# A decode-attention and MLP kernel: down-projection as partial sums per column tile, fewer VectorE instructions, and a final weight piece split by columns

## The chip, the cores and the metric

The kernel runs on one core of a Trainium2 chip. The metric is the device time of one execution in microseconds (us). A "span" is the length that the profile of one execution shows; it is 1.4 to 1.9 us shorter than the device time of the same execution. All kernels that ran gave correct results.

## The reference

```python
g = sigmoid((x * gate_w).sum(-1, keepdims=True))          # x: 8 x 1 x 576
q = x @ wq                                                 # 8 batches, 32 heads of 128
a = softmax(q @ k_cache^T * 128**-0.5) @ v_cache @ wo      # 4096 keys per head
b = gelu(layernorm(x) @ w1 + b1) @ w2 + b2                 # 576 -> 4608 -> 576
return g * a + (1 - g) * b
```

The K and V caches are the work: 2 x 8 x 32 x 4096 x 128 values in bfloat16, 537 MB of the 557 MB that the kernel reads.

## The kernel before

The kernel cuts the attention into 32 groups (eight heads of one batch each). A group needs one K load and one V load of 8.4 MB. SBUF has room for three such slots. The loads are issued by SyncE on one queue, strictly in order, and each one waits until its slot is free:

| order | load | slot | free when |
|---|---|---|---|
| 1-3 | wq, w1, w2 | 0, 1, 2 | at once |
| 4 | K0 | 0 | the q projection has read wq |
| 5 | K1 | 1 | the up-projection has read w1 |
| 6 | V0 | 2 | the down-projection has read w2 |
| 7 | K2 | 0 | TensorE has summed the last chunk of K0 |
| 8 | V1 | 1 | TensorE has summed the last chunk of K1 |
| 9 | K3 | 2 | the output of V0 has been evicted |

The order of TensorE's work at the start is: up-projection, then (after gelu on VectorE and ScalarE) 36 small matmuls that transpose the hidden row, then (after four VectorE copies of it) the down-projection, then the two matmuls that broadcast q of group 0, and only then the attention.

```python
    for k in range(3):                       # up-projection, w1 in slot 1
        for c in range(4):
            ...
    free[1] = [p_up]
    ...                                      # gelu on VectorE and ScalarE
    for j in range(NJ):                      # NJ = 36: transposes of the hidden row
        p_hT = op("tensor", ...)
    v_hT = [op("vector", lambda e, c=c: e.tensor_copy(
        out=hT_sb[32 * c:32 * c + 32, :, :], in_=ht_ps[0:32, :, c, :]), [p_hT]) for c in range(4)]

    def quarters(lhsT, w, first, stop, waits):          # 4 matmuls of 144 columns into y_ps
        for i in range(4):
            last = op("tensor", lambda e, i=i: e.matmul(
                y_ps[32 * i:32 * i + B, 0:QN], lhsT=lhsT, rhs=w[:, i * QN:(i + 1) * QN], start=first, stop=stop),
                waits if i == 0 else ())
        return last

    for jt in range(NJ):                     # down-projection, w2 in slot 2
        p_down = quarters(hT_sb[:, jt, :], w2_sb[:, jt, :], jt == 0, False, ...)
    for i in range(4):
        p_b2 = op("tensor", ...)             # bias b2 times (1 - g)
    free[2] = [p_b2]
    ...
    q_of(0)                                  # first q: 2 matmuls on TensorE, then a copy on ScalarE
    next_load()                              # K1
    next_load()                              # V0
    ...
    for g in range(NG):
        scores(g, between)                   # 8 x (VectorE multiply K by q, TensorE sums, VectorE reduce)
        free[n_of["k", g]] = [... p_sum[g, NCK - 1]]    # in the loop: a later matmul of the same point
        next_load()
        ...                                  # softmax, P @ V, eviction
```

At the end, y (already holding the MLP part) gets the wo product in three pieces of rows, `WO = ((0, 24), (24, 30), (30, 32))`, and four copies bring it to SBUF for the output.

Of the kernel before, what the change touches and what calls it, by code (L numbers as in the profile page):

```python
# [6 lines left out]
ALU = mybir.AluOpType  # L7
AX = mybir.AxisListType
BF16 = mybir.dt.bfloat16
F32 = mybir.dt.float32  # L10

B = 8
D = 576
# [6 lines left out]
NJ = F // 128  # L20

HB = 8
# [10 lines left out]
QN = D // 4  # L33
QP = 96 + B
# [3 lines left out]
NDQ = 4  # L38
NJO = H * DH // 128
# [4 lines left out]
class Stream:  # L44
# [13 lines left out]
    def op(self, engine, fn, waits=(), dma=None, token=None):  # L58

        rec = {"fn": fn, "waits": [w for w in waits if w is not None], "value": None, "inc": None, "token": None}  # L60
        self.ops[engine].append(rec)
        if dma is not None:
            rec["inc"] = (dma[0], 16)
            return ("dma", *dma)
        if token is not None:
            key = (engine, token)
            if key not in self.tok:
                self.tok[key] = self.nc.alloc_semaphore(f"tok_{engine}_{token}")
                self.given[key] = 0
            self.given[key] += 1  # L70
            rec["inc"] = (self.tok[key], 1)
            rec["token"] = (token, self.given[key])
        return ("op", engine, rec)
# [117 lines left out]
def bass_gated_mix__mha_block_cached__mixer_channel_mlp__decode_kernel(  # L191
# [16 lines left out]
    sb = nc.alloc_sbuf_tensor  # L208
    S = Stream(nc)
    op = S.op  # L210

    def pstride(t):
        return t[tuple([slice(None)] * len(t.shape))].ap[0][0]
# [16 lines left out]
    w2_sb = view(SL, 2 * SLOT, [128, NJ, D])  # L230
# [33 lines left out]
    late = Tail(2, NJ * D)  # L264
    b1_row = late.take([1, F])
    hrow = late.take([128, FC])
    hT_sb = late.take([128, NJ, B])
    b2_8 = late.take([B, D])
    b2_f = late.take32([B, D])
    t2 = late.take32([128, FC])  # L270
# [4 lines left out]
    selq = sb("selq", [128, TQ, HB * NDQ], F32)  # L275
    zs = sb("zs", [32, 1], F32)
    acc = sb("acc", [128, GL, HB], F32)
    OTs = sb("OTs", [32, NJO, GL], F32)
# [9 lines left out]
    one1 = sb("one1", [1, B], BF16)  # L288
    diag2 = sb("diag2", [B, 2, B], F32)
    g4 = sb("g4", [128, 2], F32)  # L290
    g32 = sb("g32", [32, 2, B], F32)
    ident = sb("ident", [128, 128], BF16)
    hneg = sb("hneg", [128, HB], F32)
    sel32 = sb("sel32", [128, HB, TQ], F32)
# [3 lines left out]
    mB = sb("mB", [128, 32], F32)  # L298
    mC = sb("mC", [128, 32], F32)
    mD = sb("mD", [128, 32], F32)  # L300
# [3 lines left out]
    O_sb = sb("O_sb", [128, TQ, DH], F32)  # L304
    rz = sb("rz", [128, 1], F32)

# [9 lines left out]
    g4_ps = bank[3][:, 0:2]  # L316
    g32_ps = bank[3][0:32, 64:64 + 2 * B]
    ht_ps = PS[:, 0:NJ * 32].rearrange("p (j c b) -> p j c b", j=NJ, c=4)
    xt_ps = bank[7]
    YT_COL = 64  # L320
# [4 lines left out]
    def load(engine, dst, src, name, waits=()):  # L325
        return op(engine, lambda e: e.dma_start(dst, src), waits, dma=(nc.alloc_semaphore(name), 16))
# [5 lines left out]
    def bcast(t, at, n):  # L332
        return bass.AP(tensor=t.tensor, offset=t.offset + at, ap=[[0, B], [1, n]])
# [15 lines left out]
    ld_b1 = load("scalar", b1_row, bass.AP(tensor=B_b1.tensor, offset=B_b1.offset, ap=[[F, 1], [1, F]]), "ld_b1")  # L349
    ld_b2 = load("scalar", b2_8, bcast(B_b2, 0, D), "ld_b2")  # L350

# [38 lines left out]
    def memset(engine, ap, value):  # L390
# [14 lines left out]
                                                    base=PH - 1, pattern=[[PH, HB], [0, NDQ]], channel_multiplier=-1), [t])  # L405
    c_hneg = op("vector", lambda e: e.tensor_scalar(out=hneg[:, :], in0=hsel[:, ::NDQ], scalar1=-1.0, scalar2=60000.0,
                                                    op0=ALU.add, op1=ALU.mult), [c_hsel])
# [8 lines left out]
        axis=AX.X, op=ALU.add), [c_id])  # L416
    c_selq = op("vector", lambda e: e.tensor_copy(
        out=selq[:].rearrange("p t (h q) -> p t h q", q=NDQ),
        in_=bass.AP(tensor=sel32, offset=0, ap=[[pstride(sel32), 128], [1, TQ], [TQ, HB], [0, NDQ]])), [c_sel32])
    c_one8 = memset("gpsimd", ones8[:], 1.0)  # L420
    c_one1 = memset("gpsimd", one1[:], 1.0)
    c_b2 = op("gpsimd", lambda e: e.tensor_copy(out=b2_f, in_=b2_8), [ld_b2])
    c_sp8 = op("vector", lambda e: e.tensor_copy(
        out=spread8[:].rearrange("b (c r) -> b c r", c=4),
        in_=bass.AP(tensor=ident, offset=0, ap=[[pstride(ident), B], [0, 4], [1, 32]])), [c_id])
    c_Rows = op("vector", lambda e: e.tensor_reduce(
        out=Rows[:], in_=ident[:, :].rearrange("p (h r) -> p h r", h=4), axis=AX.X, op=ALU.add), [c_id])
    c_Sel = op("vector", lambda e: e.tensor_copy(
        out=Sel[:].rearrange("p (h r) -> p h r", h=4),
# [35 lines left out]
    def untransposed(dst, col, waits):  # L465
        return op("vector", lambda e: e.tensor_copy(
            out=dst.rearrange("p k b -> p (k b)"), in_=xt_ps[:, col:col + (NKF + 2) * B]), waits)
# [8 lines left out]
                                                   scalar1=-1.0, scalar2=1.0, op0=ALU.mult, op1=ALU.add), [a_g])  # L476
    v_dg = op("vector", lambda e: e.tensor_tensor(
        out=diag2[:], in0=bass.AP(tensor=ident, offset=0, ap=[[pstride(ident), B], [0, 2], [1, B]]),
        in1=bass.AP(tensor=stat, offset=G_COL, ap=[[pstride(stat), B], [1, 2], [0, B]]), op=ALU.mult), [v_omg, c_id])
    v_yz = spread(yz, y_sb, [v_y])  # L480
# [3 lines left out]
           [v_dg, c_sp8])  # L484
    t = op("tensor", lambda e: e.matmul(g32_ps, lhsT=ones8[:, :], rhs=diag2[:].rearrange("k s b -> k (s b)"),
                                        start=True, stop=True), [c_one8])
    v_g4 = op("vector", lambda e: e.tensor_copy(out=g4[:, :], in_=g4_ps), [t])
    v_g32 = op("vector", lambda e: e.tensor_copy(out=g32[:].rearrange("p s b -> p (s b)"), in_=g32_ps), [t])

# [50 lines left out]

    def quarters(lhsT, w, first, stop, waits):

        for i in range(4):
            last = op("tensor", lambda e, i=i: e.matmul(  # L544
                y_ps[32 * i:32 * i + B, 0:QN], lhsT=lhsT, rhs=w[:, i * QN:(i + 1) * QN], start=first, stop=stop),
                waits if i == 0 else ())
        return last

    for jt in range(NJ):
        p_down = quarters(hT_sb[:, jt, :], w2_sb[:, jt, :], jt == 0, False,  # L550
                          [ld_w2, *v_hT, v_yT] if jt == 0 else ())
    for i in range(4):
        p_b2 = op("tensor", lambda e, i=i: e.matmul(
            y_ps[32 * i:32 * i + B, 0:QN], lhsT=diag2[:, 1, :], rhs=b2_f[:, i * QN:(i + 1) * QN], start=False, stop=False),
            [c_b2, v_dg])
    free[2] = [p_b2]

# [50 lines left out]
    def softmax(g):  # L608
        own = "vector" if in_loop(g) else None
        t = op("vector", lambda e: e.tensor_reduce(out=mA[:, 0:1], in_=s_sb[:, :], axis=AX.X, op=ALU.max),  # L610
               [v_red[g, NCK - 1], c_mA], token=own)
        t = op("vector", lambda e: e.transpose(mB[:, :], mA[:, :]), [t], token=own)
        t = op("vector", lambda e: e.tensor_reduce(out=gm[:, :], in_=mB[:, :].rearrange("p (k r) -> p k r", k=2),
                                                   axis=AX.X, op=ALU.max), [t], token=own)
        gmb = bass.AP(tensor=gm, offset=0, ap=[[pstride(gm), 128], [1, 2], [0, PH]])
        t = op("vector", lambda e: e.tensor_scalar(out=mC[:, :].rearrange("p (k r) -> p k r", k=2), in0=gmb,
                                                   scalar1=-1.0, scalar2=None, op0=ALU.mult), [t], token=own)
        t = op("vector", lambda e: e.transpose(mD[:, :], mC[:, :]), [t], token=own)
        v_nm[g] = op("vector", lambda e: e.tensor_scalar(out=hb8[:, :], in0=hneg[:, :], scalar1=mD[:, 0:1], scalar2=None,
                                                         op0=ALU.add), [t, c_hneg, a_exp.get(g - 1)],  # L620
                     token="scalar" if in_loop(g) else None)
# [84 lines left out]

    WO = ((0, 24), (24, 30), (30, 32))
    ld_wo = {}

    def load_wo(waits):  # L710
        w = A_wo.rearrange("(p j) n -> p j n", j=NJO)
        for n, (j0, j1) in enumerate(WO):
            t = load("sync", wo_sb[:, j0:j1, :], w[:, j0:j1, :], f"ld_wo{n}", waits)
            ld_wo.update({j: t for j in range(j0, j1)})

# [41 lines left out]
    norm(last)  # L757
    place_o("vector", last - 1, last + 1)
    for j in range(NJO):
        p_a = quarters(OT[:, j, :], wo_sb[:, j, :], False, j == NJO - 1, [ld_wo[j], *g_ot.values()])  # L760
    parts = [op("vector" if i < 2 else "scalar", lambda e, i=i: (e.tensor_copy if i < 2 else e.copy)(
        out_sb[:, i * QN:(i + 1) * QN], y_ps[32 * i:32 * i + B, 0:QN]), [p_a]) for i in range(4)]
    ld_out = [load("sync", out_flat, out_sb[:, :], "ld_out", parts)]
# [35 lines left out]
```

## Time and profile before

Three runs gave a median of 1295.15 us.

| what | value | view |
|---|---|---|
| load queue, share of the 16 DMA engines' span | 99.6% | queue table |
| mean bandwidth | 431 GB/s | page |
| VectorE, TensorE busy | 63%, 57% | busy table |
| V1's load issued | 111.47 us | timeline of SyncE |
| output issued, span | 1291.23, 1293.2 us | timeline, page |

The first lines below are from the page of the profile of before: busy time of each engine with its share of the span and its number of instructions; then, for the DMA queues, packets, megabytes and share of the 16 engines.

```profile
PE 733.4 (57%) x4926; PEld 337.1 (26%) x4926; DVE 819.7 (63%) x873; ACT 161.0 (12%) x587; POOL 40.4 (3%) x60
...
q1 hardware_dynamic: 10528, 556.94, 99.6%
q8 instruction: 9, 0.15, 0.0%
...
HBM read 556.96 MB, written 0.01 MB: 431 GB/s over the span
```

The kernel is bound by its DMA engines. The Trainium skill, "DMA: Bandwidth & Descriptors", section Specifications, gives 435 GB/s as the fabric's ceiling. The trace agrees: it shows 431 GB/s over the whole span, and 430 to 436 in the steady part.

The next fence is the timeline of before: start in us, duration in us, engine, line, operation, output and input, number of instructions, and in brackets the idle time of the engine before it with what ended it.

```profile
52.94 1.89 DVE L538 CAST SL<-PS 32x288 bf16<-32x288 f32 x4 [2.39 <-PE PS L535]
...
54.97 3.96 PE L544 MATMUL PS<-SL 128*8 128x144 bf16 x144 [2.07 <-DVE SL L538]
...
58.86 0.43 PE L553 MATMUL PS<-SL,diag 8*8 8x144 f32 x8
...
59.22 0.25 PE L569 MATMUL PS<-Qm,Sel 128*64 128x128 bf16 x2
59.34 0.33 SPq L384 DMA_DIRECT2D SL<-in_A_v_cache_dram  x1
59.50 0.28 ACT L572 ACTIVATE q_bc<-PS 128x128 bf16<-128x128 f32 x1 [10.41 <-PE PS L569]
...
59.89 4.49 DVE L580 TENSOR_TENSOR SL<-SL,q_bc 128x4096 bf16<-128x4096 bf16 x2 [5.06 <-DMA SL<-in_A_k_cache_dram]
...
84.42 0.33 SPq L384 DMA_DIRECT2D SL<-in_A_k_cache_dram  x1
111.47 0.33 SPq L384 DMA_DIRECT2D SL<-in_A_v_cache_dram  x1
```

Read it from the top as one chain: hidden row copied (L538), down-projection (L544), bias (L553), first q (L569, L572), first multiply (L580) at 59.89 us. The three SPq lines are the issues of V0, K2 and V1.

The waits of SyncE's queue in before (line that waited, what it waited for: us in total, times, longest) show what separates the last two issues from what came before them:

```profile
SPq L384 <- PE PS L585: 51.4, 2, 26.7
```

L585 is TensorE's sum over a K chunk. K2 waited for group 0 and V1 for group 1, together 51.4 us. These waits begin when V0 has been issued (59.34 us), half a microsecond before the first multiply. From that multiply to V1's issue it is 111.47 - 59.89 = 51.6 us, the time of groups 0 and 1; the table of runs below shows that this distance hardly changes. When do the DMA engines run out of earlier work? The trace keeps every DMA packet with its start, duration and size. By these, the 16 engines finish K2 between 115.56 and 117.47 us. (The landing records, which tell when each engine reports a load as done, come 0.4 us later: 115.96 to 117.91 us. A load has landed when its last engine reports.) V1 was issued 4.1 us ahead of the first of these moments. In the steady part a V load issued at 181.7 us took 33.0 us to land, of which 19.4 us were its own transfer, so 13.6 us of earlier work was queued.

The windows of before (range, length, busy time of PE, PEld, DVE, ACT, POOL, then TensorE's granted clock, DMA share, GB/s), and the DMA issues view (us from issue to landing, here of V1):

```profile
110.00:125.00 15.00, 9.76 (x87) 4.68 (x85) 8.13 (x12) 4.52 (x17) 3.36 (x1) 0.89 1.01 434
116.00:119.00 3.00, 0.00 (x0) 0.00 (x0) 1.06 (x1) 3.00 (x13) 0.00 (x0) 1.00 0.87 371
27.00:45.00 18.00, 15.60 (x72) 5.42 (x72) 2.00 (x2) 0.00 (x0) 0.00 (x0) 0.88 1.01 434
```

The end of before, from its timeline:

```profile
1290.22 0.30 PE L544 MATMUL PS<-SL,OT 128*8 128x144 bf16 x8 [0.21 <-DMA SL<-in_A_wo_dram]
...
1290.57 0.63 DVE L761 CAST out_sb<-PS 8x144 bf16<-8x144 f32 x2 [3.50 <-PE PS L544]
1291.23 0.37 SPq L326 DMA_DIRECT2D out_dram<-out_sb  x1
```

The last piece of wo lands at 1290.18 us (landing records); 1.05 us later the output is issued.

### The profile page before, as it was taken

Reading aid. Unit: us, or ns where it says so; the run is one execution under the profiler, and the core shown is the slowest. Engines: PE = TensorE matmul, PEld = TensorE weight load, DVE = VectorE, ACT = ScalarE, POOL = GpSimd, SP = SyncE. Lnnn points to the kernel's source line nnn. Section 1 sums busy time; section 2 is a strip of 40 time slices with the busy share of each in tenths; the row PEclk is TensorE's granted clock in tenths of the full one; section 3 lists DMA queues with packets and bytes.
Section 4 is the critical chain, followed back from the end, with each engine's and each line's share of the span. In section 5 each row is a group of like instructions: output and inputs, shape, how many; then the busy total and the mean of one; then the engine's idle time right before and its main releaser. Section 6 shows DMA issues by size and latency. Waiting matters only on the chain.

```text
span 1293.2 us, 11790 instructions
## 1 busy us (share of the span) xinstructions
PE 733.4 (57%) x4926; PEld 337.1 (26%) x4926; DVE 819.7 (63%) x873; ACT 161.0 (12%) x587; POOL 40.4 (3%) x60
## 2 busy tenths in 40 slices
PE   3666566555556555556555556555556555556646
PEld 1322223122223222223222223222223222223223
DVE  2387567665567665567665567765567765567762
ACT  1011110111110011110011110011111011111011
POOL 1001000000000000000000000000000000000000
PEclk8799898878898887898787899778888877888888
DMA  9999999999999999999999999999999999999998
GB/s 406 427 447 424 439 430 436 432 430 436 434 428 436 436 432 438 430 438 432 430 436 434 428 436 438 430 438 430 438 430 432 436 432 434 432 438 430 436 424 366
DMA packets 10591, 557.16 MB, mean 431 GB/s; under 512 B 1201, under 2 KB 1233, under 8 KB 1745
## 3 DMA queue, kind: packets, MB, share of 16 engines
q1 hardware_dynamic: 10528, 556.94, 99.6%
q8 instruction: 9, 0.15, 0.0%
q10 hardware_dynamic: 50, 0.04, 0.0%
q14 instruction: 4, 0.03, 0.0%
HBM read 556.96 MB, written 0.01 MB: 431 GB/s over the span
## 4 chain that ended last, share of the span: by engine, by line
DMA 54%; DVE 26%; PE 14%; ACT 5%; issue 1%; SPq 0%; ACTq 0%; DVEq 0%
DMA SL<-in_A_k_cache_dram 50%; DVE SL L580 20%; PE PS L585 7%; DVE s_sb L591 5%; ACT P L625 4%; PE PS L640 4%; DMA SL<-in_B_w_dram 2%; DMA SL<-in_A_wo_dram 2%; PE PS L515 1%; PE PS L656 1%; ACT O_sb L645 1%; PE PS L544 0%; PE PS L518 0%; PE PS L649 0%; PE PS L535 0%
## 5 line engine op out<-in xcount | busy, mean ns | idle before, releaser
L585 PE MATMUL PS<-SL,ident 128*128 128x512 bf16 x2048 | 547.7, 420 | 518.3 <-DVE SL L580 518.3
L580 DVE TENSOR_TENSOR SL<-SL,q_bc 128x4096 bf16<-128x4096 bf16 x256 | 582.0, 2284 | 313.6 <-DMA SL<-in_A_k_cache_dram 313.6
L585 PEld LDWEIGHTS PS<-SL,ident 128*128 128x128 bf16 x2048 | 199.0, 106 | 853.8 <-DVE SL L580 614.8
L591 DVE TENSOR_REDUCE s_sb<-PS 128x32 f32<-128x512 f32 x256 | 175.8, 687 | 90.4 <-PE PS L585 90.3
L625 ACT ACTIVATE P<-s_sb,hb 128x256 bf16<-128x256 f32 x256 | 126.2, 494 | 663.3 <-PE PS L640 645.5
L640 PE MATMUL PS<-SL,P 128*32 128x512 bf16 x2048 | 128.5, 389 | 0.0
L640 PEld LDWEIGHTS PS<-SL,P 128*32 128x32 bf16 x2048 | 96.4, 138 | 17.9 <-issue 3.1
L564 POOL TENSOR_SCALAR Qm<-Q,sel 128x256 bf16<-128x256 bf16 x33 | 33.7, 1020 | 896.6 <-ACT O_sb L645 845.2
L572 ACT ACTIVATE q_bc<-PS 128x128 bf16<-128x128 f32 x33 | 9.1, 277 | 407.4 <-PE PS L569 407.4
L625 ACT ACTIVATION_READ_ACCUMULATOR P<-s_sb,hb 128x1 f32 x256 | 47.7, 186 | 0.0
L656 PE MATMUL PS<-O_sb,selq 128*32 128x128 f32 x256 | 34.2, 278 | 0.7 <-ACT O_sb L645 0.7
L656 PEld LDWEIGHTS PS<-O_sb,selq 128*32 128x32 f32 x256 | 26.0, 113 | 1.4 <-ACT O_sb L645 1.2
L645 ACT ACTIVATE O_sb<-PS 128x512 f32<-128x512 f32 x32 | 18.4, 574 | 10.0 <-PE PS L640 10.0
L523 DVE COPY SL<-PS 104x1152 f32<-104x1152 f32 x1 | 1.4, 1357 | 28.7 <-PE PS L518 28.7
L515 PE MATMUL PS<-SL 128*8 128x384 bf16 x60 | 13.2, 356 | 6.8 <-DMA SL<-in_B_w_dram 6.8
L669 DVE SCALAR_TENSOR_TENSOR On<-PS,rz,dqm 32x128 f32<-32x128 f32 x32 | 10.9, 339 | 9.0 <-PE PS L656 7.9
L683 POOL TENSOR_TENSOR OT<-OTs,g 32x96 bf16<-32x96 f32 (+2 forms) x12 | 4.2, 347 | 320.3 <-DVE OTs L673 320.2
L610 DVE TENSOR_REDUCE mA<-s_sb 128x1 f32<-128x256 f32 x32 | 13.4, 420 | 1.1
L673 DVE TENSOR_REDUCE OTs<-On 32x32 f32<-32x128 f32 x32 | 12.1, 378 | 1.1
L649 PE MATMUL PS<-acc,hsel 128*32 128x8 f32 x64 | 7.4, 188 | 5.9 <-ACT O_sb L645 4.7
L663 DVE TENSOR_REDUCE zs<-PS 32x1 f32<-32x8 f32 x32 | 4.7, 147 | 8.2 <-PE PS L656 7.9
L649 PEld LDWEIGHTS PS<-acc,hsel 128*32 128x32 f32 x64 | 4.5, 110 | 19.5 <-issue 12.7
(82 smaller groups left out, 114.5 us busy)
## 6 DMA issues: line engine op xcount, KB each, us to landing
SL<-in_A_v_cache_dram SPq DMA_DIRECT2D x2, 4096.0 KB, 38.4
SL<-in_B_w_dram SPq DMA_DIRECT2D x1, 5184.0 KB, 37.7
SL<-in_B_w_dram SPq DMA_DIRECT2D x1, 4608.0 KB, 24.1
SL<-in_A_wq_dram SPq DMA_DIRECT2D x1, 4096.0 KB, 13.0
SL<-in_A_wo_dram SPq DMA_DIRECT2D x1, 3456.0 KB, 22.0
SL<-in_A_wo_dram SPq DMA_DIRECT2D x1, 864.0 KB, 23.7
SL<-in_B_w_dram SPq DMA_DIRECT2D x1, 576.0 KB, 25.0
SL<-in_A_wq_dram SPq DMA_DIRECT2D x1, 512.0 KB, 13.6
```

Of the source, the lines that this page charges most:

```text
L515: p_up = op("tensor", lambda e, o=o, r=r, kt=kt, yi=yi: e.matmul(o, lhsT=yT_sb[:, yi, :], rhs=r, start=(kt == 0), stop=False), [v_yT, *ld_ ...
L564: g_qm[g] = op("gpsimd", lambda e: e.tensor_scalar(out=Qm[:, :, :].rearrange("p k d -> p (k d)"), in0=Q4[:, 2 * hg * DH:(2 * hg + 2) * DH] ...
L580: v_mult[g, c] = op("vector", lambda e: e.tensor_tensor(out=part, in0=part, in1=qb, op=ALU.mult), [land["k", g], a_qb[g]], token="tensor" ...
L585: p_sum[g, c] = op("tensor", lambda e, r=r, n=n: e.matmul(tr_ps[par][:, :], lhsT=ident[:, :], rhs=r, start=(n == 0), stop=(n == NCH - 1)), ...
L591: v_red[g, c] = op("vector", lambda e: e.tensor_reduce(out=s_sb[:, c * CT:(c + 1) * CT], in_=tr_ps[par][:, :].rearrange("p (t c) -> p t c" ...
L610: t = op("vector", lambda e: e.tensor_reduce(out=mA[:, 0:1], in_=s_sb[:, :], axis=AX.X, op=ALU.max), [v_red[g, NCK - 1], c_mA], token=own)
L625: a_exp[g] = op("scalar", lambda e, h=h: e.activation(out=P[:, :, h, :], in_=s_sb[:, :].rearrange("p (s t) -> p s t", s=2), func=ACT.Exp, ...
L640: p_pv[g] = op("tensor", lambda e, o=o, lhsT=lhsT, rhs=rhs, tq=tq: e.matmul(o, lhsT=lhsT, rhs=rhs, start=(tq < 4), stop=(tq >= NTQ - 4)), ...
L645: a_ev[g] = op("scalar", lambda e: e.activation(out=O_sb[:].rearrange("p t d -> p (t d)"), in_=o_ps[:, :], func=ACT.Copy), [p_pv[g], p_z.g ...
L649: p_z[g] = op("tensor", lambda e: e.matmul(oz_ps[0:32, DH:DH + HB], lhsT=hsel[:, :], rhs=acc[:, place(g), :], start=True, stop=True), [a_e ...
L656: p_oz[g] = op("tensor", lambda e, tt=tt: e.matmul(oz_ps[0:32, 0:DH], lhsT=selq[:, tt, :], rhs=O_sb[:, tt, :], start=(tt == 0), stop=(tt = ...
L673: v_norm[g] = op("vector", lambda e: e.tensor_reduce(out=OTs[:, :, place(g + 2)], in_=On[:, :].rearrange("p (q j) -> p j q", q=NDQ), axis= ...
```

## The change

The change has three parts. The down-projection streams w2 in 288 columns into four partial sums, one per column tile of TensorE, in place of 144 matmuls of 144 columns; VectorE then adds the bias in one instruction, and four float32 matmuls add the four sums up. VectorE loses a negation per group and seven small set-up copies, which ScalarE takes over. The last piece of wo is split by columns, so that half of the output can be copied while the other half is multiplied.

```diff
-    for jt in range(NJ):
-        p_down = quarters(hT_sb[:, jt, :], w2_sb[:, jt, :], jt == 0, False,
-                          [ld_w2, *v_hT, v_yT] if jt == 0 else ())
+    for j0 in range(0, NJ, 4):
+        for k in range(2):
+            for c in range(4):
+                jt = j0 + c
+                p_down = op("tensor", lambda e, jt=jt, k=k, c=c: e.matmul(
+                    b_ps[32 * c:32 * c + B, k, 0:D // 2], lhsT=hT_sb[:, jt, :], rhs=w2_sb[:, jt, k * (D // 2):(k + 1) * (D // 2)],
+                    start=(jt < 4), stop=(jt >= NJ - 4)), [ld_w2, *v_hT, v_h] if jt == k == 0 else ())
+    v_b = op("vector", lambda e: e.scalar_tensor_tensor(
+        out=b_sb[0:QP, :]..., in0=b2_z[0:QP, :]...,
+        scalar=g4[0:QP, 1:2], in1=b_ps[0:QP, :, 0:D // 2], op0=ALU.mult, op1=ALU.add), [p_down, ld_b2, v_g4])
     for i in range(4):
-        p_b2 = op("tensor", lambda e, i=i: e.matmul(
-            y_ps[...], lhsT=diag2[:, 1, :], rhs=b2_f[:, i * QN:(i + 1) * QN], start=False, stop=False), [c_b2, v_dg])
-    free[2] = [p_b2]
+        p_y = op("tensor", lambda e, i=i: e.matmul(
+            y_ps[...], lhsT=sel32[0:QP, :, :]..., rhs=b_sb[0:QP, i * QN:(i + 1) * QN], start=True, stop=False), [v_b, v_yT, c_sel32])
+    free[2] = [p_y]
# ... cut: in softmax, per group
-        t = op("vector", lambda e: e.tensor_scalar(out=mC[:, :]..., in0=gmb, scalar1=-1.0, ...), [t], token=own)
-        t = op("vector", lambda e: e.transpose(mD[:, :], mC[:, :]), [t], token=own)
+        t = op("vector", lambda e: e.transpose(mD[:, :], gmb), [t], token=own)
# ... cut: seven set-up copies from "vector" to "scalar"; the tail
-    WO = ((0, 24), (24, 30), (30, 32))
+    WO = ((0, 24, 0, 4), (24, 31, 0, 4), (31, 32, 2, 4), (31, 32, 0, 2))
-        p_a = quarters(OT[:, j, :], wo_sb[:, j, :], False, j == NJO - 1, [ld_wo[j], *g_ot.values()])
+        for i in range(4) if j < NJO - 1 else (2, 3, 0, 1):
+            p_a[i] = op("tensor", lambda e, i=i, j=j: e.matmul(...), [ld_wo[j, i], *g_ot.values()])
-    parts = [... [p_a]) for i in range(4)]
+    parts = [... [p_a[i]]) for i in (2, 3, 0, 1)]
```

## The prediction

> **What bounds it.** The DMA engines, from about 2 us to 1290 us. The queue table gives the load queue 99.6% of the 16 engines' span; windows between 120 and 280 us show 430 to 436 GB/s. The Trainium skill, "DMA: Bandwidth & Descriptors", section Specifications, puts the fabric ceiling at 435 GB/s; the trace agrees. No compute engine is near that (VectorE 63%, TensorE 57% by the busy table). The chain of waits runs through VectorE and TensorE for half its length, but loads are issued long before the engines run dry: a V load issued at 181.7 us lands 33.0 us later; at 19.4 us of transfer each, 13.6 us of earlier work was still queued ahead of it. VectorE idles about 10 us per group, waiting for K.
>
> **What the change does.**
> 1. Down-projection (timeline, 54.9 to 59.3 us): 144 matmuls of 144 columns, 3.96 us, plus 0.43 us for b2, become 72 matmuls of 288 columns, a VectorE combine (about 0.75 us, estimated as half the 1.35 us of the 104x1152 op that reads PSUM), and four fp32 matmuls of 0.4 us. The granted clock was 0.5 to 0.7 here, so streaming 72x288 columns over four column tiles takes about what 144x144 took: estimate 3 to 4.3 us. Net: first q up to 1.5 us later. V0's load, issued at 59.3 us, could come as late as 79 us (K1's landing) without an idle DMA engine: worth 0 on the total.
> 2. VectorE: 32 negations of 0.18 us go (5.8 us), and seven small setup copies move to ScalarE. All before 15 us or inside a loop that waits for K data: 0. x's transpose copy now queues behind two ScalarE activations; Q starts at 15 us when wq lands, so at most a few tenths there, again behind 14 us of queued weights.
> 3. Tail, the only critical part. Before: last wo piece lands 1290.18, 8 matmuls 0.33 us, two serial copies 0.63 us, output issued 1291.23, end 1293.2. After: two pieces of one row-group, half the columns each. In the DMA records a 2304-byte descriptor takes 93 ns and a 6912-byte one 262 ns, so about 8.5 ns each is fixed; eight extra descriptors per engine, and a semaphore write of 9 ns, delay the last landing by about 0.08 us (estimate). The middle piece grows from 6 to 7 rows: it lands 0.34 us later (about 1289.8), and its 28 matmuls (24 took 0.55 us) end near 1290.4, when both last pieces have nearly landed. So only part of the hoped overlap comes: four matmuls' less wait, columns 2-3 copied perhaps 0.1 us before columns 0-1 are ready; the second copy still queues behind the first. Gain about 0.1 us, at most 0.4.
>
> **Total.** 1295.0 us (range 1294.2 to 1295.9; the three runs before span 1.3 us). Faster by over 2%: 0.005; within 2%: 0.99; slower: 0.005.
>
> **What would show it.** Load queue still 99.6%, about 431 GB/s; VectorE busy down some 7 us, idle up as much; V0's issue within 2 us of 59.3; last wo landing 1290.1 to 1290.5; output issue 1290.8 to 1291.3.
>
> **What would make it wrong.** The 16-KB instruction fetches of about 1.07 us share these DMA engines (nine in the trace, each on a different engine by my reading); a shifted program could put two on one engine, or take one off the slowest: plus or minus 1 us. A small-descriptor cost above my estimate would add tenths.

## More of the kernel before

In the rounds that also ran the changed kernel, before gave 1295.09 us (six runs, 1294.69 to 1296.36).

The bracket of the first multiply names the landing of K0: q is ready just as K0 arrives, so neither waits for the other.

Reckoned as for V1, from the issue to the first engine that is done with the load before, V1 has 4.1 us, and every other K or V load of this trace after K1 has 11.2 us or more.

```profile
SL<-in_A_v_cache_dram SPq DMA_DIRECT2D x1, 25.8
```

A caution about this view: it counts a packet whole in the window in which it starts, and a packet of these loads takes 2.42 us, so a window of a few microseconds can show too much or too little. The 371 GB/s of the second line is such an effect. The packets themselves follow one another without a pause on all 16 engines; spread over their durations they give 432 GB/s for 110 to 125 us. V1 landed at 111.47 + 25.8 = 137.3 us.

## The result, and the profile after

The changed kernel took 1296.24 us (median of six runs: 1294.89, 1295.45, 1296.06, 1296.41, 1296.93, 1298.08) beside 1295.09 us for before in the same rounds. The ratio is 1.0008, with a 95% interval of 0.9995 to 1.0021. Ratios here and below are the mean time of one kernel's runs over that of the other's of the same rounds, so they are not quite the ratio of the medians quoted. All outputs are right. The class is "within 2%", as predicted, but the median lies 0.3 us above the predicted range of 1294.2 to 1295.9 us.

Two facts warn against reading a single run here. The interval includes 1, and some runs of the changed kernel are as quick as any of before. A second set of five runs (label after_again) gave 1296.76 us and the same ratio of 1.0008.

The page of the changed kernel, lines as above:

```profile
PE 734.9 (57%) x4854; PEld 334.7 (26%) x4854; DVE 813.6 (63%) x835; ACT 163.6 (13%) x595; POOL 37.8 (3%) x60
...
q1 hardware_dynamic: 10672, 556.94, 99.5%
q8 instruction: 8, 0.13, 0.0%
...
HBM read 556.96 MB, written 0.01 MB: 430 GB/s over the span
```

VectorE did get 6.1 us lighter. The queue is as full as before to a tenth of a per cent; but a tenth of a per cent of 1295 us is 1.3 us, so on this page the effect hides in the last digit. The timeline of the changed kernel at the start:

```profile
54.72 1.89 DVE L537 CAST SL<-PS 32x288 bf16<-32x288 f32 x4 [2.40 <-PE PS L534]
...
56.76 4.49 PE L544 MATMUL PS<-SL 128*8 128x288 bf16 x72 [2.07 <-DVE SL L537]
61.30 0.81 DVE L547 SCALAR_TENSOR_TENSOR SL<-SL,g,PS 104x576 f32<-104x576 bf16 x1 [4.69 <-PE PS L544]
...
62.16 0.67 PE L551 MATMUL PS<-SL,sel 104*8 104x144 f32 x8 [0.92 <-DVE SL L547]
...
62.76 0.32 PE L567 MATMUL PS<-Qm,Sel 128*64 128x128 bf16 x2
62.89 0.33 SPq L385 DMA_DIRECT2D SL<-in_A_v_cache_dram  x1
63.12 0.28 ACT L570 ACTIVATE q_bc<-PS 128x128 bf16<-128x128 f32 x1 [12.25 <-PE PS L567]
...
63.50 4.50 DVE L578 TENSOR_TENSOR SL<-SL,q_bc 128x4096 bf16<-128x4096 bf16 x2 [1.39 <-ACT q_bc L570]
...
88.28 0.33 SPq L385 DMA_DIRECT2D SL<-in_A_k_cache_dram  x1
114.84 0.33 SPq L385 DMA_DIRECT2D SL<-in_A_v_cache_dram  x1
```

The first multiply now waits for q (the bracket names q_bc, no longer K0) and starts 63.50 - 59.89 = 3.6 us later. K2's and V1's issues are 3.9 and 3.4 us later. The waits of SyncE's queue say that the distance itself did not change:

```profile
SPq L385 <- PE PS L583: 51.3, 2, 26.2
```

Windows of the changed kernel at the same places, and V1's time from issue to landing:

```profile
110.00:125.00 15.00, 11.39 (x98) 5.25 (x98) 12.22 (x14) 4.80 (x18) 0.92 (x1) 1.00 1.01 411
116.00:119.00 3.00, 2.42 (x48) 1.40 (x40) 1.91 (x5) 0.46 (x2) 0.00 (x0) 1.00 0.65 240
27.00:45.00 18.00, 17.50 (x72) 5.65 (x72) 0.25 (x1) 0.00 (x0) 0.00 (x0) 0.78 1.01 434
```

```profile
SL<-in_A_v_cache_dram SPq DMA_DIRECT2D x1, 24.2
```

This is where the time went. The view shows 411 GB/s between 110 and 125 us and not 434. With each packet spread over its duration it is 398 against 432 GB/s, which is 15 us x 34/432 = 1.2 us of transfer lost on the average engine. The last engine, which decides when the load has landed, lost more: V1 lands at 114.84 + 24.2 = 139.0 us, 1.8 us later than before (landing records: 139.08 against 137.27 us). Since the queue is full from then on, nothing gives these microseconds back: the last V load lands 1.9 us later (1271.30 against 1269.38 us), and the span is 2.0 us longer (1295.2 against 1293.2).

The packets of the same trace show three things at V1's start. Its first packet moved at 115.80 us, 0.96 us after its issue began. By then the first engines had already run dry (they finished K2 from 115.5 us on). And the first descriptors were slow: a 65,536-byte descriptor takes 2.42 us in the steady part, while 27 of those that began between 115.8 and 119.8 us took 2.6 to 3.5 us. Third, the two engines that were last to finish K2 (117.2 and 117.5 us) began V1 only at 118.2 and 118.5 us, on average 1.0 us later, although V1 had been issued more than two microseconds before; their first descriptors then took 3.5 and 3.4 us. These pauses of about 1.0 us and descriptors of about 1.0 us too much account for the late landing. Why an engine pauses or slows down there, no run shows. A load normally lands 19.36 us after the one before it; V1 landed 21.17 us after K2.

The end of the changed kernel:

```profile
1291.70 0.68 PE L759 MATMUL PS<-SL,OT 128*8 128x144 bf16 x32 [0.73 <-DMA SL<-in_A_wo_dram]
1292.40 0.63 DVE L762 CAST out_sb<-PS 8x144 bf16<-8x144 f32 x2 [4.01 <-PE PS L759]
...
1293.09 0.37 SPq L326 DMA_DIRECT2D out_dram<-out_sb  x1
```

The 28 matmuls of the middle piece and the four of the last row run as one block of 32, because the middle piece lands only about 0.4 us before the last one (landing records: about 1292.07 us). From the last landing to the output's issue it is 1.02 us, against 1.05 us before. The split by columns gained 0.03 us in this run.

### The profile page after: what moved, and what is told of

The parts are those of the page before. It is cut to its first block, busy times and chain, and to the rows that moved or that the text cites. A ratio compares the mean times of both kernels' runs of the same rounds, so it can differ in the third digit from the quotient of the medians. Undisturbed runs are those within 1.5% of the kernel's fastest.

```text
span 1295.2 us, 11619 instructions
## 1 busy us (share of the span) xinstructions
PE 734.9 (57%) x4854; PEld 334.7 (26%) x4854; DVE 813.6 (63%) x835; ACT 163.6 (13%) x595; POOL 37.8 (3%) x60
## 3 DMA queue, kind: packets, MB, share of 16 engines
q1 hardware_dynamic: 10672, 556.94, 99.5%
## 4 chain that ended last, share of the span: by engine, by line
DMA 53%; DVE 26%; PE 15%; ACT 5%; issue 1%; SPq 0%; ACTq 0%; DVEq 0%
DMA SL<-in_A_k_cache_dram 50%; DVE SL L578 20%; PE PS L583 7%; DVE s_sb L589 5%; ACT P L621 4%; PE PS L636 4%; DMA SL<-in_B_w_dram 2%; DMA SL<-in_A_wo_dram 2%; PE PS L514 1%; PE PS L652 1%; ACT O_sb L641 1%; PE PS L544 0%; PE PS L517 0%; PE PS L645 0%; PE PS L534 0%
```

## The experiments

Theory A: the change makes q of group 0 later; the delay passes in full through groups 0 and 1 to V1's issue, which comes too late for a queue that is about to run dry. Rival B: the finer tail pieces or their descriptors cost the time. Rival C: the shifted program, or another of the small moves, costs it. Rival D: V0's later issue itself starves the queue.

The expectations use other letters: their S is theory A, their T is B, their C is chance in the clock alone, and their N is a spread that has nothing to do with V1's load.

Fourteen runs were made besides the two above; one of them, after_again, is the changed kernel once more. This table gathers what the trace of each shows; "V1's interval" is the time from K2's landing to V1's (landing records), and "after" is the changed kernel in the profile shown above. The other kernels (e4 to e7) issued V1 by 111.6 us and have no long V1 load.

| kernel | first multiply | V1 issued | V1's interval | span |
|---|---|---|---|---|
| before | 59.89 | 111.47 | 19.36 | 1293.2 |
| after | 63.50 | 114.84 | 21.17 | 1295.2 |
| after_again | 61.42 | 113.26 | 19.34 | 1294.3 |
| e1_down_undone | 60.01 | 111.34 | 19.31 | 1294.0 |
| e2_down_only | 63.65 | 115.28 | 20.36 | 1294.7 |
| dose2 | 63.50 | 115.20 | 20.18 | 1294.9 |
| dose3 | 63.73 | 115.19 | 20.30 | 1294.1 |
| dose5 | 70.34 | 122.01 | 24.49 | 1301.8 |
| e3_hoist | 59.47 | 110.26 | 19.44 | 1293.3 |
| e8_warm | 63.06 | 114.39 | 20.38 | 1294.4 |
| e9_warm_long | 59.97 | 111.72 | 19.35 | 1293.3 |
| e10_before_warm_long | 63.30 | 115.26 | 21.29 | 1295.1 |

Every traced run that issued V1 by 111.8 us has a normal V1 interval; every one that issued it at 114.39 us or later has 20.2 to 24.5 us. The distance from first multiply to V1's issue is 50.8 to 52.0 us in this table. Among the six runs from 114.39 to 115.28 us the loss does not follow the issue time (20.18 to 21.29 us).

The span mixes two things, and the landing records part them. The last V load of the whole kernel landed at 1269.3 to 1269.5 us in all eight traced runs that issued V1 by 111.8 us, at 1270.4 to 1271.4 us in the seven that issued it from 113.26 to 115.28 us, and at 1277.3 us in dose5. So what is lost at V1 is still missing at the end. The rest of the differences in span comes mostly from the end of the kernel: from the last landing of wo to the end of the span the traces show 3.0 to 3.9 us, the longer ones (from 3.4 us) all with TensorE at half clock for the wo matmuls. That is why e1_down_undone has a span of 1294.0 us with a normal V1 load.

### Undo the down-projection, or do it alone

Label e1_down_undone is the changed kernel with the old 144 matmuls into y_ps; everything else of the change stays (the bias is scaled by VectorE during the up-projection).

```diff
-    for j0 in range(0, NJ, 4):        # 72 matmuls of 288 columns into b_ps, then v_b behind them
+    for jt in range(NJ):              # 144 matmuls of 144 columns into y_ps
+        for i in range(4):
+            p_down = op("tensor", lambda e, i=i, jt=jt: e.matmul(y_ps[32 * i:32 * i + B, 0:QN], ...))
     for i in range(4):
-        p_y = op("tensor", ... start=True, stop=False), [v_b, v_yT, c_sel32])
+        p_y = op("tensor", ... start=False, stop=False), [v_b, v_yT, c_sel32])
```

> The changed kernel with its down-projection put back to four quarters straight into the output bank (b2's share added from a row scaled early), all else as changed. Theory S (start-up chain: the new down-projection makes the first multiply later, so the load of V1 is issued at about 114.8 us instead of 111.5 us, just as the DMA engines run dry): V1's load issued at 111 to 113 us, no load of 8.4 MB takes more than 19.4 us from landing to landing, time 1295.1 us within 0.4, narrow spread. Rival T (the split tail costs the time): stays near 1296.2 us. Rival C (chance in the clock alone): a spread as wide as the changed kernel's, 1294.9 to 1298.

Measured: 1295.29 us (1294.98 to 1295.71), before 1295.08 us in the same rounds, ratio 0.9998 (0.9984 to 1.0012). The first multiply is back at 60.01 us and V1's issue at 111.34 us, with a normal V1 load. The tail, the moved copies and the shifted program of the change are all in this kernel, and none of its five runs was slow. This speaks against B and C, though five runs are few: of before's own 43 runs only 13 were slow (counted below).

Label e2_down_only is before with the new down-projection and its bias load alone.

> The kernel before with the new down-projection alone. Theory S: V1's load issued after 113.5 us, in some runs after 114.6 us, median 1295.5 to 1297 us, runs up to 1298. Rival T: 1295.1 us as before. Rival C: no different from before.

Measured: 1294.56, 1294.73, 1294.77, 1296.33 and 1298.18 us; median 1294.77, ratio 1.0001 (0.9987 to 1.0014). The median missed the expectation: three of the five runs lost nothing. The traced run did as expected: first multiply at 63.65 us, V1 issued at 115.28 us, an interval of 20.36 us. So the down-projection brings the late V1 load, but not in every run. Something that differs from run to run decides with it, which the clock experiments below take up.

### Doses of delay

These are before, with the four copies of the hidden row done two, three or five times over. One pass is 1.89 us of VectorE in front of the down-projection. Nothing of the change is in them.

```diff
-    v_hT = [op("vector", ..., [p_hT]) for c in range(4)]
+    v_hT = [None] * 4
+    for r in range(5):                # dose2: 2, dose3: 3
+        v_hT = [op("vector", ..., [p_hT, v_hT[c]]) for c in range(4)]
```

> The kernel before with the four VectorE copies that feed its down-projection made three times over, one after another: 3.8 us more in the start-up chain, nothing else changed. Theory S: V1's load issued at about 115.3 us; idle DMA engines plus a slow restart, 1296 to 1297.5 us. Rivals T and C: 1295.1 us, as the work added is before 60 us and the load queue is full then.

> As the run with three copies, but five: 7.6 us more in the start-up chain. Theory S: V1's load issued at about 119 us, 4.5 us beyond the last harmless moment of 114.6 us, and a slow restart of up to 1 us: 1299 to 1301 us. Rivals T and C: 1295.1 us.

> The kernel before with the four VectorE copies twice: 1.9 us more in the start-up chain, between the kernel before and the run with three copies (median 1297.0 us). Theory S: V1 issued at about 113.4 us in runs with the high clock (loss 0 to 1 us, part of it from slow first descriptors) and 116 us in those with the low one (loss 2 to 3.5 us): median 1295.2 to 1296.5 us, several runs above 1296.2. Rival N: as the kernel before.

| kernel | added | median (range) | ratio to before (95%) |
|---|---|---|---|
| dose2 | 1.9 us | 1296.36 (1296.20 to 1299.56) | 1.0012 (0.9998 to 1.0025) |
| dose3 | 3.8 us | 1297.00 (1295.63 to 1299.21) | 1.0018 (1.0004 to 1.0031) |
| dose5 | 7.6 us | 1301.37 (1300.87 to 1304.24) | 1.0049 (1.0036 to 1.0063) |

A pure delay in front of the first q costs time, in an otherwise untouched kernel. Beyond the slack the cost of the medians grows about one for one: dose5 has 3.8 us more than dose3 and takes 4.4 us more. The traced runs do not have this spacing: dose5's first multiply is 6.6 us later than dose3's, and dose2's is as late as dose3's but for 0.2 us, since the traces drew different clocks before the copies (see below). dose5's V1 was issued 3 us later than expected, and its median is 0.4 us above the expected range. In the trace of dose5 the queue really runs dry; its timeline and a window:

```profile
122.01 0.33 SPq L384 DMA_DIRECT2D SL<-in_A_v_cache_dram  x1
```

```profile
117.00:122.00 5.00, 3.82 (x20) 1.49 (x24) 3.62 (x4) 0.00 (x0) 0.00 (x0) 1.00 0.00 0
```

In these five microseconds no packet of data started. By the packets, the engines finished K2 between 116.5 and 119.4 us and began V1 at 122.97 us, so for 3.5 us all 16 loaded nothing. dose5 shows one thing more: K2 was issued at 94.9 us, about 1.2 us before the first engine needed it. Yet four engines began K2 late (3.7 us of pause together), its first descriptors took up to 4.1 us, and its interval was 21.17 us. In these traces a load has to be on the queue some microseconds ahead, not merely in time: V1 of e9_warm_long, issued 3.8 us before the first engine needed it, started without loss, V1 of after_again, 2.2 us before, did not.

### The first q ahead of the down-projection

Label e3_hoist is the changed kernel with all its parts, but the first q is computed before the down-projection, and the combine of the partial sums is put behind the first two multiplies of group 0.

```diff
+    q_of(0)
     v_hT = [op("vector", ...) for c in range(4)]
+    p_down = down()                   # the 72 matmuls as in the change
 ...
         mult(g, 1)
+        if g == 0:
+            combine(p_down)           # v_b, the four float32 matmuls, free[2]
+            next_load()               # K1
+            next_load()               # V0
         between(1)
 ...
-    q_of(0)
```

> The changed kernel with the first group's q made before the down-projection, and the combine of the four partial sums put behind the first two multiplies, so that the first multiply waits for K0 alone. Theory S (start-up chain too close to the moment when the DMA engines run dry; how close depends on the change by about 1 us and on the clock granted to TensorE by about 3 us): first multiply at 59 to 60 us in any clock state, V1 issued by 112 us, no long load, all runs 1294.5 to 1295.3 us. Rival T (the tail costs the time): still a median near 1296 us. Rival N (spread of the chip that has nothing to do with V1's load): spread as the changed kernel's.

Measured: 1295.37 us (1294.85 to 1295.66) beside 1295.18 us of before, ratio 0.9997 (0.9983 to 1.0010). Its timeline: the first multiply, then the issues of V0, K2 and V1; and a window.

```profile
59.47 4.49 DVE L586 TENSOR_TENSOR SL<-SL,q_bc 128x4096 bf16<-128x4096 bf16 x2 [2.14 <-DMA SL<-in_A_k_cache_dram]
...
66.34 0.33 SPq L385 DMA_DIRECT2D SL<-in_A_v_cache_dram  x1
83.47 0.33 SPq L385 DMA_DIRECT2D SL<-in_A_k_cache_dram  x1
110.26 0.33 SPq L385 DMA_DIRECT2D SL<-in_A_v_cache_dram  x1
```

```profile
27.00:45.00 18.00, 17.93 (x71) 5.71 (x71) 0.00 (x0) 0.00 (x0) 0.00 (x0) 0.73 1.01 434
```

Three of the five runs lie above the 1295.3 us that was expected as the highest, but none above 1295.7 us. This run decides against D. V0 is issued at 66.34 us, later than in the changed kernel (62.89 us), and nothing is lost; what came earlier is the first multiply, and with it V1's issue. The window shows that the up-projection of this run had a slower clock (0.73) than the changed kernel's (0.78) and ended no earlier. The first multiply no longer depends on that.

The changed kernel itself was run again beside it.

> The changed kernel again, unchanged, beside the others on one chip, to see how much of its first 1296.24 us was chance. Theory S: two kinds of runs, near 1294.8 us and from 1296 to 1298 us, by the clock in the first 70 us; in the profile a V1 issue before 113.5 us goes with no long load, one after 114.4 us with a load 1 to 2 us longer than 19.36 us. Rival T: all runs 1296 us or more.

Measured: 1296.76 us (1295.60 to 1297.67), ratio 1.0008 (0.9994 to 1.0021). The expected two kinds of runs are not there: none of the five is near 1294.8 us. The traced run, too, departs from the simple picture. V1 was issued at 113.26 us, between the two camps of the table, and V1's last engine landed on time (19.34 us). But the middle one of the 16 engines landed 0.9 us late, so the quicker engines had lost their lead. Two later loads then took 20.05 and 19.71 us, each right after a 16 KB instruction fetch on one engine (at 165 and 190 us). That the lost lead and the fetches together made the 1 us is read from the trace; no run tests it.

### The tail alone, and attempts at a better version

Label e4_tail_only is before with the new pieces of wo and the new order of copies, nothing else.

```diff
-    WO = ((0, 24), (24, 30), (30, 32))
+    WO = ((0, 24, 0, 4), (24, 31, 0, 4), (31, 32, 2, 4), (31, 32, 0, 2))
```

> The kernel before with the last wo piece split by columns, alone. Theory S: as before, 1294.9 to 1295.2 us in the median, with its rare slow runs; from the last landing of wo to the issue of the output 1.0 us against 1.05 us. Rival T: 1296 us.

Measured: 1295.13 us (1294.98 to 1296.33), before 1295.18 us, ratio 0.9997 (0.9983 to 1.0010). The tail neither costs nor gains a visible amount, which speaks against B. The traces show a small cost: in the kernels with the new tail (e7 apart, which the profile does not fully explain) the span ends 0.74 us after the landing of the output, in those with the old one 0.60 us. What these 0.14 us are is open. The traced end was longer than expected: the last piece landed at about 1290.12 us and the output was issued at 1291.70 us, 1.58 us later and not 1.0. TensorE had half its clock there, and the 128 wo matmuls took 3.66 us in one block, where before at full clock needed 1.68 + 0.55 + 0.30 us.

Label e5_best is e3_hoist with the pieces (0,24), (24,30) and then the last two rows by halves of columns.

```diff
-    WO = ((0, 24, 0, 4), (24, 31, 0, 4), (31, 32, 2, 4), (31, 32, 0, 2))
+    WO = ((0, 24, 0, 4), (24, 30, 0, 4), (30, 32, 2, 4), (30, 32, 0, 2))
```

> The third kernel of this call's first run (first q early) with wo cut so that the middle piece keeps its six rows and both last pieces hold two rows of half the columns: two pieces 0.37 us apart instead of 0.2 us. Theory S: all runs within 1294.2 to 1294.9 us, from the last landing of wo to the issue of the output 0.6 to 0.8 us. If the copies are not what bounds the tail: 1.0 us as now.

Measured: 1295.20 us (1294.81 to 1295.48), ratio 0.9995 (0.9981 to 1.0008). Four of the five runs lie above the expected 1294.2 to 1294.9 us. The end missed its expectation again, and again at half clock: 1.42 us from landing to output.

Label e6_before_early_q is before with one move: the first q ahead of the down-projection. No other line differs.

```diff
+    q_of(0)
     v_hT = [op("vector", ...) for c in range(4)]
 ...
-    q_of(0)
```

> The kernel before with the first group's q made ahead of its own down-projection, nothing else. Theory S, widened (the slow runs of the kernel before, 1296.2 to 1297.8 us in 9 of 24, have the same cause: V1's load too late when TensorE's clock is low in the first 60 us): first multiply at 59 to 60 us, V1 issued by 112 us, all five runs 1294.6 to 1295.7 us. Rival N (those slow runs have another cause): about two of five runs still above 1296.2 us.

Measured: 1295.15 us (1294.50 to 1295.39) beside 1295.82 us for before (1294.84 to 1296.52), ratio 0.9994 (0.9980 to 1.0008). V1 was issued at 110.07 us. The first multiply, at 59.68 us, is hardly earlier than in before's traced run, because K0 lands only then. If there is a gain, it is that slow runs are gone, not that the quick ones are quicker. Five runs alone do not show it, since only one of the nine of before in the same rounds was slow; the count over all kernels with an early q says more (below). The expectation counts 9 slow runs of before in 24; the record has 8 from 1296.2 us on.

Label e7_best2 is e5_best with wo in six pieces, and P @ V of the last group put ahead of other end work.

```diff
-    WO = ((0, 24, 0, 4), (24, 30, 0, 4), (30, 32, 2, 4), (30, 32, 0, 2))
+    WO = ((0, 12, 0, 4), (12, 22, 0, 4), (22, 28, 0, 4), (28, 31, 0, 4), (31, 32, 2, 4), (31, 32, 0, 2))
```

> First q early, the last weighted sum of V moved ahead of the previous group's normalization, and wo in six pieces (12, 10, 6, 3 rows, then the last row in two halves), so that TensorE has no stock of wo rows left when the last piece lands even at half clock. Theory S: all runs 1294.2 to 1295.2 us; from the last landing of wo to the output's issue 0.7 to 0.9 us, where the kernel with two-row last pieces took 1.4 us at half clock. If the backlog is not what held that tail: 1.3 us or more again at half clock.

Measured: 1295.82 us (1295.50 to 1296.00), before 1295.82 us, ratio 1.0001 (0.9987 to 1.0014). A miss: half clock once more at the end, and 0.4 us between the end of the copies and the output's issue that the profile does not explain.

### The clock of TensorE

What differs from run to run? The Trainium skill, "TensorE: Matmul & The Clock Gate", part 1 (The HAM clock gate), says that TensorE's clock has two states, half and full, decided in windows of about 3.4 us that run freely, so that the same kernel meets them at a different phase each time. The traces agree: the granted clock is 0.5 or 1.0 and changes at multiples of 3.41 us. During the up-projection (27 to 45 us) it averaged 0.88 in before and 0.78 in the changed kernel, with the same matmuls: their busy time was 15.60 and 17.50 us in the windows shown above.

I tried to hold the clock up with matmuls of no use on a free PSUM bank, between the q projection and the up-projection.

```diff
     free[0] = [p_Q]
     load_kv("k", 0)
+    for i in range(116):              # e8_warm: 56
+        op("tensor", lambda e: e.matmul(bank[2][:, 128:256], lhsT=ident[:, :], rhs=ident[:, :], start=True, stop=True))
```

> The changed kernel, with 56 matmuls whose result nobody reads put on TensorE between the q projection and the arrival of w1 (about 20 to 27 us), where it idled. Theory S with the clock as the switch: TensorE works on w1 at the full clock from its start, the up-projection ends near 41 us instead of 43 to 45 us, the first multiply is at 60 to 61 us in every run, V1 issued by 112.5 us, and no run is above 1295.8 us (the changed kernel: 7 of 11 above 1296.1). Rival: if the clock at the start does not decide, the spread stays as it was, 1295 to 1298 us.

Measured: 1297.03 us (1296.02 to 1298.59), ratio 1.0012 (1.0000 to 1.0025). The 56 fillers ended at 23.7 us and the clock had fallen to half at 27.1 us, before the bulk of the up-projection. The run did not test what it was meant to.

> The changed kernel with 116 filler matmuls from about 20.4 us to w1's arrival at 27.3 us. If the clock is the switch: full clock from 27 to 41 us, up-projection done by 41.5 us (43 to 45 us until now), first multiply at 59.8 to 61 us, V1 issued by 112.5 us, all runs 1294.5 to 1296 us. If the clock falls to half all the same, the run again tests nothing. If the clock is full and V1 early, but runs above 1296.1 us remain, the clock is not what makes them slow.

> The kernel before with the same 116 filler matmuls. If the clock is the switch: V1 issued at 111 to 112 us, all runs 1294.5 to 1295.7 us, none of the slow runs that the kernel before has beside it. Else: one or two of five above 1296.1 us.

With 116 fillers, e9_warm_long (in the changed kernel) took 1297.12 us (1295.00 to 1297.89), ratio 1.0013 (0.9999 to 1.0027); e10_before_warm_long (in before) took 1296.57 us (1296.02 to 1296.86), ratio 1.0005 (0.9991 to 1.0019). Both missed their expectations: four of five runs of each lie above 1296.1 us. As a tool the fillers failed: they did not hold the clock reliably. In e9's trace it stayed full from 19.8 to 43.6 us, in e10's it fell to half at 29.2 us. For the eight untraced runs no clock is known, so these times decide nothing about it. The traced runs are informative all the same, because they drew opposite clocks. The window over the up-projection, first of e9_warm_long, then of e10_before_warm_long:

```profile
27.00:45.00 18.00, 13.95 (x72) 5.16 (x72) 2.83 (x3) 0.00 (x0) 0.00 (x0) 0.96 1.01 437
```

```profile
27.00:45.00 18.00, 16.48 (x71) 5.45 (x71) 0.00 (x0) 0.00 (x0) 0.00 (x0) 0.81 1.01 434
```

The changed kernel's code with a clock of 0.96 issued V1 at 111.72 us, had a normal V1 load and a span of 1293.3 us, as good as before. Before's code with 0.81 issued V1 at 115.26 us, had an interval of 21.29 us and a span of 1295.1 us, as poor as the changed kernel. So in the traced runs it is the moment of the first multiply that decides, whatever makes it late.

### How much is the change, how much the clock

From the start of the hidden row's copies to the q copy on ScalarE, by timelines, sorted by the clock in that stretch:

| clock | old down-projection | new down-projection |
|---|---|---|
| half, then full for the last 1.0 to 2.3 us | 6.56 (before), 6.60 (e1) | 7.70 (after_again), 7.53 (e9) |
| half throughout | 7.41 (e10) | 8.40 (after), 8.40 (e2) |

Only the second row compares like with like: at half clock the change costs 8.40 - 7.41 = 1.0 us. In the first row the difference is 0.9 to 1.1 us, but the full clock lasts 1.0 to 1.3 us in the old kernels and 2.1 to 2.3 us in the new ones. In the two profiles compared, 3.6 us lay between the first q of the two kernels: 1.8 us had already arisen in front of the copies (54.72 against 52.94), where the kernels do the same work at a different clock, and 1.8 us in this stretch (8.40 - 6.56), of which 1.0 us is the change and 0.8 us (7.41 - 6.56) the clock.

The slack can be estimated from the numbers above. The first engine is done with K2 at 115.5 us, and the first packet of a load moves 0.96 us after its issue begins, so V1 must be issued by about 114.5 us; it follows the first multiply by about 51.5 us; so the first multiply must start by about 63.0 us, and before had about 3.1 us in hand in its traced run. e8_warm (V1 issued at 114.39 us, 1.0 us lost) and after_again, at 61.42 us, show that losses begin sooner than this estimate.

Across all rounds, the share of runs above 1296.1 us (a line that I drew after seeing the data) rises with the delay: early first q (e3, e5, e6, e7) 0 of 20; before 13 of 43; new down-projection (after, after_again, e2) 9 of 16; dose2 5 of 5. Left out of this row: e1 0 of 5, e4 1 of 5, dose3 4 of 5, dose5 5 of 5, e8 5 of 6, e9 4 of 5 and e10 4 of 5. The last is far more than before's share, and whether the fillers themselves have a part in it is not tested. None of 20 against 13 of 43 is hard to get by chance (about 1 in 300, if the runs are independent); 9 of 16 against 13 of 43 is not (about 1 in 16). So the times alone leave open that the changed kernel merely drew worse clocks than before; the 1.0 us that the traces show at like clock does not depend on that. That the slow runs of the untraced executions come from an unlucky clock is an argument from the traced ones. No untraced run shows its clock of these microseconds.

## Why the prediction was right or wrong

| point of the prediction | measured | verdict |
|---|---|---|
| within 2% | ratio 1.0008 | right |
| 1295.0 us, 1294.2 to 1295.9 | 1296.24 | wrong, 0.3 us above the range |
| load queue 99.6%, 431 GB/s | 99.5%, 430 GB/s | right, and too coarse to show the loss |
| VectorE some 7 us lighter, worth 0 | 6.1 us lighter; e1 keeps it, no gain seen | right |
| combine 0.75 us, float32 matmuls 0.4 us | 0.81 us; 0.67 us at half clock (0.43 in after_again) | about right |
| first q up to 1.5 us later | 1.0 us at like clock, 3.6 us between the two profiles | right for the change, the clock not foreseen |
| V0's issue within 2 us of 59.3 | 62.89 | wrong |
| the later first q and V0 load "worth 0 on the total" | 1.1 us between the medians; in the two profiles V1's load lands 1.8 us late | wrong, the step that failed |
| middle piece delays the block; tail gains about 0.1 us, at most 0.4 | one block of 32 matmuls, gain 0.03 us at full clock; at half clock the end takes 1.4 to 1.7 us with either tail | right, the clock not foreseen |
| last landing 1290.1 to 1290.5, output issue 1290.8 to 1291.3 | 1292.07, 1293.09 | wrong, both by the late V1 load |

The step that failed reads: "V0's load, issued at 59.3 us, could come as late as 79 us (K1's landing) without an idle DMA engine: worth 0 on the total." For V0's own load this is true; e3_hoist issues it at 66.34 us at no cost. The mistake was to stop at the load whose slot the changed code frees. The same code stands, in order, in front of the first q. So it delays groups 0 and 1, and with them the slots of K2 and V1. V1 is the load with the least reserve: issued 4.1 us before the first engine runs dry, not 20 us. The number 13.6 us, which the prediction took from the steady part and applied to the whole run, does not hold for the first two groups: their compute starts only when K0 and q are there, 59.9 us into the run, and then takes 51.5 us before V1 can be issued.

The second thing missed is the clock as a source of spread. The prediction saw a clock of 0.5 to 0.7 in the down-projection and used it to size the matmuls. It did not ask what another draw would do. Because before has only about 3 us in hand and another draw of the clock can take 2.5 to 3.4 us (the share of it in 3.6 us, and e10_before_warm_long's first multiply against before's), 1 us more tips many runs over. With before's clock the 1 us alone would have fitted into the slack: e9_warm_long, the changed code with a good draw, issued V1 at 111.72 us and took 1295.00 us in its traced run, inside the predicted range. So the median's miss by 0.3 us took the failed step and the luck of the draw together, and the forecast of "within 2%" could not fail by an effect of this size.

The warning in the prediction about instruction fetches on the DMA engines was not the main cause: e1_down_undone and e3_hoist run shifted programs too and lose nothing. In after_again they seem to have a part.

## What to carry to other kernels

In a kernel bound by loads, work out the reserve load by load at the start: when does each slot become free, and when do the DMA engines run out? The reserve of the steady part says nothing about the first groups, and what is lost there is not made up in a queue that stays full. Work that frees a slot may also stand in front of other work on the same in-order engine; follow a delay through every later slot, and put the short path to the first use (here two matmuls and a copy for q) ahead of side work that nobody waits for. Putting the first q first (e6_before_early_q) is the move I would keep: it does not beat before measurably, but none of the 20 runs of the four kernels with it was slow.

## What the Trainium skill lacked or had wrong

- "DMA: Bandwidth & Descriptors", section Specifications, gives a first-byte latency of about 0.6 us for loads issued by SyncE. The trace shows 0.96 us from the start of V1's issue to its first packet, 0.63 us from the end of that issue (which takes 0.33 us), so the figure agrees if counted from the end. What no page gives is the cost of a queue that nearly runs dry: first descriptors of 2.6 to 3.5 us (dose5: up to 4.1 us) in place of 2.42 us, and 0.8 to 1.9 us on the load's landing, even where the load was issued 1.2 us before the first engine needed it (K2 in dose5).
- The same page, section "Where 436 GB/s comes from", lets the HBM side (about 358 GB/s) bind transfers from HBM to SBUF. Here one core read 431 GB/s from HBM over the whole span. "Perfetto Trace Analysis", section Roofline, has it right for a core that runs alone, with about 435 GB/s, so the sentence about the HBM side needs that condition.
- "Runtime: NRT & Kernel Launch", section "Instruction fetch mechanics", says that instructions are refilled in 16 KiB blocks over a DMA queue of the sequencer's own, and calls the cost mostly hidden. The trace shows these 16,384-byte packets on the engines that carry the loads, 1.0 to 1.1 us each, nine in before. In a kernel bound by these engines that need not stay hidden: after_again's two longer loads (20.05 and 19.71 us) each came right after such a fetch, though no run tests the link.
- "TensorE: Matmul & The Clock Gate", part 1, puts the ramp at less than 1% of a typical span and advises against fitting a model to a specific count of slow matmuls. Here the draw moved V1's issue by 3.1 us (111.72 against 114.84 us, e9_warm_long against the changed kernel) and by 3.8 us (115.26 against 111.47 us, e10_before_warm_long against before), and the span by 1.9 us both times, in code that differs only by the fillers; the granted clock over the up-projection was 0.96 against 0.78 and 0.81 against 0.88. That is under 1%, but it is the whole effect under study. The page also does not say whether matmuls of no use hold the clock up across a gap: 116 of them held it in one traced run and not in the other.
